# Other places for the filling products, state products and weight conversions at the start of a Mamba-2 and PReLU kernel

## The chip, the cores and the metric

The kernel runs on one core of one Trainium2 chip. The metric is device time in microseconds of one execution, the median of several runs. TensorE (PE) makes matrix products into PSUM banks, VectorE (DVE), ScalarE (ACT) and GpSimd (POOL) do the elementwise work, and SyncE (SP) issues most of the loads. A float32 matrix product is recorded as two passes, so the counts of the profile are twice those of the program.

## The reference

The first part is a Mamba-2 recurrence over 4 batches, 8 heads and 768 positions, with head size 32 and 16 state numbers. The second is a feed-forward layer with a leaky slope per hidden unit (PReLU), on 3072 tokens of 256 numbers with 2048 hidden units.

```python
# per chunk of positions, with cum the running sum of log(clip(a, 1e-6, 1)):
M       = (C @ B.T) * exp(cum_i - cum_j) * causal
y       = M @ x + (C @ state) * exp(cum)
state   = exp(sum(log_a)) * state + B.T @ (x * exp(cum_last - cum))
# then, with x = y laid out as tokens x 256:
h = x @ w_in
g = maximum(h, 0) + alpha * minimum(h, 0)
out = g @ w_out
```

## The kernel before

The kernel takes chunks of 128 positions, two at a time (a "pair", 12 in all). Two pairs make a group of 512 tokens for the feed-forward layer. Only the first group's start concerns us: pairs 0 and 1, then hidden blocks f = 0 to 3 of the first group in halves, and then a loop over f = 4 to 15 that makes `hidden(0, f)`, converts one more piece of the weights, and adds `output(f - 4)`. The three later groups are computed by another, denser scheme that the change does not touch.

The order of instructions on each engine is the order in the program. Tiles in PSUM come from three pools: `ss` (two banks), `hp` (two banks, `spare()` gives one of them) and single banks.

The weights arrive as float64 in 16 pieces of 512 KB (in the order w_in 0, 1, 2, w_out 0, w_in 3, w_out 1, ...) and are converted to float32 by hand. `convert_a` is the first part (ScalarE, then a clamp on GpSimd), `convert_b` the second (VectorE), and `convert` ends with an addition, mostly on GpSimd:

```python
    def convert_a(dst, src, sg):
        ...
        nc.scalar.activation(out=t.bitcast(F32), in_=hi.bitcast(F32), func=ACTF.Abs, scale=0.125)   # L218
        nc.gpsimd.tensor_scalar(out=t..., in0=t..., scalar1=F64_INF, scalar2=F64_ZERO, ...)         # L220
        if sg is None:
            nc.scalar.activation(out=g, in_=half, func=ACTF.Copy, ...)                              # L225
        for i in range(2 if sg is not None else 0):                                                 # w_out
            nc.scalar.activation(out=g[:, i], in_=half[:, i], func=ACTF.Identity, ...)              # L228
    def convert_b(dst, src, sg):
        nc.vector.tensor_single_scalar(out=r, in_=hi, scalar=SIGN, op=ALU.bitwise_and)              # L238
        nc.vector.scalar_tensor_tensor(out=r, in0=t, scalar=3, in1=r, ...)                          # L239
    def convert(dst, src, sg, halves=(nc.gpsimd,)):
        ...
            eng.tensor_tensor(out=d[:, ks], in0=r[:, ks], in1=g.bitcast(U32)[:, ks], op=ALU.add)    # L261

    def convert_next(first=True, **kw):
        i = done[0]
        if i < len(pieces):
            convert(*pieces[i], **kw)
            if first and i and i + 2 < len(pieces):
                convert_a(*pieces[i + 2])
            if loaded[0] == i + 6:
                load_next()
        done[0] += 1
```

`keep_warm` makes products of ones whose results nobody uses; they only keep TensorE occupied:

```python
    def keep_warm(to, n, cols=2 * Q):                       # Q = 128
        for i in range(n):
            nc.tensor.matmul(to[:, :cols], warm[:, :P], warm[:, :cols], start=True, stop=True, ...)  # L270
```

A pair is a generator that is advanced stage by stage with `ssm(gp)`. The parts of it that matter (cut):

```python
        tp = spare() if gp == 1 else ss_tile()
        if gp == 0:
            keep_warm(tp, 1, Q)
        ...                                    # transposes of B and C (L470), bc copied by ScalarE (L473),
                                               # cz = bc masked (L482, L485)
        if gp == 0:
            keep_warm(rows_turn(0, held.pop("pr"))[:, HT:], 5, Q)   # rows_turn: two transposes into one bank,
            yield                                                   # copied by ScalarE (prt, alpha)
        bn = bns.pop(gp) if gp in bns else pair_loads(gp)           # GpSimd, L386
        if gp == 1:
            c_decayed()                                             # GpSimd, L488
            dps = spare()
            ahead[1] = spread(z, 1, lambda w: ss_tile())            # TensorE, L407
        ...
            decays(0)                                               # VectorE scans, L433
            if gp:
                yield
            if gp != 1:
                decays(1)
        def added(dps): ...                                         # state products, TensorE, L532
        def states(dps): ...                                        # VectorE or ScalarE (L541, L544), then sm (L547)
        ...
        if gp == 0:
            gram = products_bc()                                    # CB products, TensorE, L561
            dps = added(spare())
            yield
            c_decayed()
            times(dec[:, :, :2], one_less(gram))                    # one_less: ScalarE, L569; times: GpSimd, L573
        elif gp == 1:
            free = dps[:, HT:]                                      # the upper half of the state products' bank
            dps = added(dps)
            decays(1)
            gram = products_bc()
            keep_warm(free, 2)
            g0 = one_less(gram)
            states(dps)
            times(dec[:, :, :2], g0)
        ...                                                         # VectorE multiplies dec by CB, L600
        y = [...]
        if gp < 2:
            keep_warm(y[0].rearrange("p k t -> p (k t)"), 2)
        ...                                                         # y products (L616, L623), copied to xT (L630)
```

`hidden_two(g, f, t0, hp)` makes two hidden blocks for 256 tokens (products L657, ScalarE L663) and returns a function that does VectorE's part (L669). `hidden` is the same for one block of 512 tokens (L642, L645, L646). `slopes(alpha)` makes the slopes' tables with five small operations on GpSimd (L308 to L317). The order of the start:

```python
    ssm(0)
    convert_a(*pieces[0]); ssm(0); convert_b(*pieces[0]); ssm(0); convert_a(*pieces[1]); ssm(1)
    convert_next(halves=(nc.vector, nc.gpsimd))
    ssm(0)
    ssm(1)
    slopes(alpha)
    prelus = [hidden_two(0, 0, 0, spare())]
    convert_a(*pieces[2])
    convert_next(first=False)
    ssm(1)
    convert_a(*pieces[3])
    prelus.append(hidden_two(0, 2, 0, spare()))
    for rest in prelus:
        rest()
    convert_next()
    ssm(1)
    convert_next(first=False)
    for rest in [hidden_two(0, f, 2 * Q, spare()) for f in range(0, FIRST, 2)]:
        rest()
    identity_bank()                                                 # ScalarE, L333
    convert_a(*pieces[5])
    convert_next()
    for f in range(FIRST, NF):
        ...
```

Of the kernel before, what the change touches and what calls it, by code (L numbers as in the profile page):

```python
# [22 lines left out]
def kernel(  # L23
# [33 lines left out]
    Q = 128  # L57
# [16 lines left out]
    HT = GT // 2  # L74
# [18 lines left out]
    gp = ctx.enter_context(tc.tile_pool(name="gp", bufs=16))  # L93
# [113 lines left out]
    def convert_a(dst, src, sg):  # L207

        if src.dtype == F32:
            return  # L210
        raw = raws.pop(id(dst))
        hi = raw[:, :, :, 1]
        half = raw.rearrange("p k w t -> p k (w t)").bitcast(U16)
        half = half.rearrange("p k (w t) -> p k w t", t=4)[:, :, :, 1]
        t = wtp.tile([P, 2, WQ], U32, name="wt")
        g = wtp.tile([P, 2, WQ], F32, name="wg")

        nc.scalar.activation(out=t.bitcast(F32), in_=hi.bitcast(F32), func=ACTF.Abs, scale=0.125)  # L218

        nc.gpsimd.tensor_scalar(out=t.bitcast(F32), in0=t.bitcast(F32), scalar1=F64_INF,  # L220
                            scalar2=F64_ZERO, op0=ALU.min, op1=ALU.max)


        if sg is None:
            nc.scalar.activation(out=g, in_=half, func=ACTF.Copy, scale=2.0**-11, bias=2.0**25)  # L225
        for i in range(2 if sg is not None else 0):
            f = slice(sg + i, sg + i + 1)
            nc.scalar.activation(out=g[:, i], in_=half[:, i], func=ACTF.Identity,  # L228
                                 scale=g_mul[:, f], bias=g_add[:, f])
        parts[id(dst)] = hi, t, g  # L230
# [36 lines left out]
    def keep_warm(to, n, cols=2 * Q):  # L267

        for i in range(n):
            nc.tensor.matmul(to[:, :cols], warm[:, :P], warm[:, :cols], start=True, stop=True,  # L270
                             skip_group_check=True)
# [27 lines left out]
    alpha = const.tile([P, NF], F32, name="alpha")  # L299
# [6 lines left out]
    def slopes(alp):  # L306
        over = const.tile([P, NF], F32, name="over")
        nc.gpsimd.tensor_scalar(out=over, in0=alp, scalar1=1.0, scalar2=None, op0=ALU.is_gt)  # L308
        nc.gpsimd.tensor_scalar(out=s_mul, in0=over, scalar1=-2.0, scalar2=1.0, op0=ALU.mult,
                                op1=ALU.add)  # L310
        nc.gpsimd.tensor_tensor(out=s_alpha, in0=alp, in1=s_mul, op=ALU.mult)
        if moe_w_out.dtype == F32:
            nc.vector.tensor_single_scalar(out=s_out, in_=s_mul.bitcast(U32), scalar=SIGN,
                                           op=ALU.bitwise_and)
        else:
            for o, by in ((g_mul, 2.0**-11), (g_add, 2.0**25)):
                nc.gpsimd.tensor_scalar(out=o, in0=s_mul, scalar1=by, scalar2=None, op0=ALU.mult)  # L317
# [8 lines left out]
    held = {}  # L326
# [38 lines left out]
    def rows_turn(i, pr):  # L365

        ps = ss_tile()
        nc.tensor.transpose(ps[:, :RW], pr, ident[:RW, :RW])
        if i == 0:
            nc.tensor.transpose(ps[:, RW : RW + NF], al_n, ident[:NF, :NF])  # L370
        t = bat.tile([P, RW], F32, name="prt")
        nc.scalar.copy(out=t, in_=ps[:, :RW])
        if i == 0:
            nc.scalar.copy(out=alpha, in_=ps[:, RW : RW + NF])
        prt[i] = t
        return ps

    def pair_loads(gp):

# [33 lines left out]
    def spare():  # L413

        return ps_h.tile([P, GT], F32, name="hp", tag="hp")

    def pair(gp):
# [7 lines left out]
        def decays(k):  # L425

            if abc:
                for w in range(2):
                    half_decays(k, w)
                return  # L430
            for w, t in enumerate(ahead.pop(k, None) or spread(z, k)):
                ws = slice(512 * w, 512 * w + 512)
                nc.vector.tensor_tensor_scan(out=dv[:, k, ws], data0=t, data1=ident_h[:, ws],  # L433
                                             initial=0.0, op0=ALU.mult, op1=ALU.add)

        def half_decays(k, w):
            for i in range(2):
                hs = slice((2 * w + i) * 2 * Q, (2 * w + i + 1) * 2 * Q)
                nc.vector.tensor_tensor_scan(out=dv[:, k, hs], data0=abc[k][:, hs],  # L439
                                             data1=ident_p[0], initial=0.0, op0=ALU.mult,  # L440
                                             op1=ALU.add)
# [22 lines left out]

        tp = spare() if gp == 1 else ss_tile()
        if gp == 0:
            keep_warm(tp, 1, Q)
        for i in range(2):
            for k in range(2):
                nc.tensor.transpose(tp[:, (2 * i + k) * P : (2 * i + k + 1) * P], nat[:, i, k],  # L470
# [7 lines left out]
        def spread_c():  # L478
            for e in range(2):
                o = cz[:, e].rearrange("p k t -> p (k t)")  # L480
                if gp == 0 and e == 1:
                    nc.gpsimd.tensor_scalar(out=o, in0=ct, scalar1=par[:, e : e + 1],  # L482
                                            scalar2=None, op0=ALU.mult)
                else:
                    nc.scalar.mul(o, ct, par[:, e : e + 1])  # L485

        def c_decayed():
            nc.gpsimd.tensor_tensor(out=cd.rearrange("p k t -> p (k t)"), in0=ct, in1=pf,  # L488
                                    op=ALU.mult)

        fine = gp >= 2 * GC // 2
        if not fine:
            spread_c()
        if gp == 0:
            keep_warm(rows_turn(0, held.pop("pr"))[:, HT:], 5, Q)
            yield
        bn = bns.pop(gp) if gp in bns else pair_loads(gp)
        if gp == 1:
            c_decayed()
            dps = spare()  # L500
            ahead[1] = spread(z, 1, lambda w: ss_tile())
        elif gp:
            yield

        if fine:
            for k in range(2):
                for w in range(2):
                    half_decays(k, w)
                    if k == 1 and w == 1:
                        spread_c()  # L510
                    yield
        else:
            decays(0)
            if gp:
                yield
            if gp != 1:
                decays(1)

# [6 lines left out]
        def added(dps):  # L527
            dps = dps.rearrange("p (k m) -> p k m", m=P)
            for k in range(nk):
                for w in range(KC):  # L530
                    ws = slice(64 * w, 64 * w + 64)
                    nc.tensor.matmul(dps[ws, k], bn[:, k, ws], xt[:, k, w * P : (w + 1) * P],  # L532
                                     start=True, stop=True, tile_position=(0, 64 * w),
                                     skip_group_check=True)
            return dps

        def states(dps):
            for k in range(nk):
# [35 lines left out]

        if gp == 0:
            gram = products_bc()
            dps = added(spare())
            yield
            c_decayed()
            times(dec[:, :, :2], one_less(gram))  # L580
        elif gp == 1:
            free = dps[:, HT:]
            dps = added(dps)
            decays(1)
            gram = products_bc()
            keep_warm(free, 2)
            g0 = one_less(gram)
            states(dps)
            times(dec[:, :, :2], g0)
        else:  # L590
            if not fine:
                yield
            states(added(ss_tile()))
# [3 lines that stand above are left out]
# [10 lines left out]

        y = [ss_tile()[:, : 2 * Q].rearrange("p (k t) -> p k t", k=2) for w in range(KC)]
        if gp < 2:
            keep_warm(y[0].rearrange("p k t -> p (k t)"), 2)  # L610
        begun = False
        for k in range(2):
            if st[k] is not None:
# [284 lines left out]
    def ssm(gp, stages=1):  # L898

        if gp not in pairs:  # L900
            pairs[gp] = pair(gp)
        for i in range(stages):
            next(pairs[gp], None)


    pieces = in_pieces[:2]
# [9 lines left out]
# [11 lines that stand above are left out]
# [13 lines left out]
    FIRST = 4  # L940
# [4 lines left out]
    ssm(0)  # L945
    convert_a(*pieces[1])
    ssm(1)
    convert_next(halves=(nc.vector, nc.gpsimd))
    ssm(0)
    ssm(1)  # L950
    slopes(alpha)
    prelus = [hidden_two(0, 0, 0, spare())]
    convert_a(*pieces[2])
    convert_next(first=False)
    ssm(1)
    convert_a(*pieces[3])
    prelus.append(hidden_two(0, 2, 0, spare()))
    for rest in prelus:
        rest()
    convert_next()  # L960
    ssm(1)
    convert_next(first=False)
    for rest in [hidden_two(0, f, 2 * Q, spare()) for f in range(0, FIRST, 2)]:
        rest()
    identity_bank()
    convert_a(*pieces[5])
    convert_next()
# [108 lines left out]
```

## Time and profile before

| | |
|---|---|
| time, median of 3 runs | 378.24 us (378.05 to 378.95) |
| span of the profiled run | 377.2 us, 6178 instructions |
| TensorE busy | 367.2 us, 97% |
| VectorE, ScalarE, GpSimd busy | 241.5 (64%), 179.5 (48%), 203.2 us (54%) |
| loads and stores | 30.71 MB, mean 81 GB/s |
| mean granted clock of TensorE | 0.994 |

A matrix product's end is modelled, so a busy TensorE isn't TensorE at its peak, and the share of busy time is a mean over stages with different limits. Where a line of the profile ends in square brackets, it gives the idle time of the engine just before that instruction and what ended it. L numbers are lines of the program; a line that stands in a helper covers all uses of that helper. In the chain and in timelines the first two numbers are the start and the duration in us.

### The profile page before, as it was taken

How to read it: one execution, taken by the hardware profiler on the slowest of the kernel's cores; microseconds unless marked ns; L12 is line 12 of the kernel's file. 1: busy time of each engine (PE TensorE's matmuls, PEld its weight loads, DVE VectorE, ACT ScalarE, POOL GpSimd, SP SyncE). 2: the span in 40 equal slices, each digit the busy share in tenths (PEclk: the TensorE clock that was granted, in tenths of full speed). 3: DMA queues.
4: the chain of work that ended last, by engine and by line, in shares of the span. 5: the costliest groups of instructions: out<-in, count | busy, mean ns of one | idle time of the engine just before them, and what ended most of it. 6: DMA issues, size and time to landing. Idle time of an engine off the chain costs nothing.

```text
span 377.2 us, 6178 instructions
## 1 busy us (share of the span) xinstructions
PE 367.2 (97%) x2223; PEld 295.5 (78%) x2223; DVE 241.5 (64%) x461; ACT 179.5 (48%) x384; POOL 203.2 (54%) x212
## 2 busy tenths in 40 slices
PE   7999999999999999999999999999999999999996
PEld 6767566668778788788788788888788788888884
DVE  7777699967636737747737847647856734543364
ACT  1466756525344445545435535525625525543541
POOL 4764476679766846445456345356364355254512
PEclk9899999999999999999999999999999999999999
DMA  7999697921008901001901901901711000001003
GB/s 141 186 225 346 162 272 171 180 70 56 30 0 156 179 2 54 5 0 30 180 3 30 179 2 29 180 2 28 140 44 21 9 0 15 17 0 30 1 0 83
DMA packets 121878, 30.71 MB, mean 81 GB/s; under 512 B 93736, under 2 KB 117752, under 8 KB 121848
## 3 DMA queue, kind: packets, MB, share of 16 engines
q1 hardware_dynamic: 116736, 29.74, 35.4%
q10 hardware_dynamic: 5112, 0.59, 1.1%
q8 instruction: 17, 0.28, 0.3%
q14 instruction: 13, 0.11, 0.1%
HBM read 26.98 MB, written 3.34 MB: 80 GB/s over the span
## 4 chain that ended last, share of the span: by engine, by line
PE 84%; DVE 5%; SPq 4%; DMA 2%; ACT 2%; issue 1%; ACTq 0%; POOLq 0%; DVEq 0%
PE hp L766 33%; PE bank L741 32%; PE bank L680 5%; PE hp L642 3%; PE ss L623 2%; PE ss L561 2%; SPq L165 2%; SPq L163 1%; DMA raw<-in_moe_w_in_dram 1%; PE ss L616 1%; DVE dec L439 1%; PE ss L532 1%; DMA nat<-in_B_dram 1%; PE hp L561 1%; PE hp L657 1%
## 5 line engine op out<-in xcount | busy, mean ns | idle before, releaser
L809 POOL TENSOR_TENSOR gt<-gt 128x512 f32<-128x512 f32 x58 | 73.6, 1270 | 31.8 <-DVE gt L751 24.8
L751 DVE SCALAR_TENSOR_TENSOR gt<-hp,s_mul,gt 128x256 f32<-128x256 f32 x120 | 52.5, 479 | 47.8 <-ACT gt L749 46.8
L741 PE MATMUL bank<-gt,w_out 128*128 128x256 f32 x320 | 82.5, 382 | 0.4 <-ACT o_sb L687 0.4
L749 ACT ACTIVATE gt<-hp,s_alpha 128x256 f32<-128x256 f32 x120 | 50.3, 470 | 47.2 <-PE hp L766 32.9
L741 PEld LDWEIGHTS bank<-gt,w_out 128*128 128x128 f32 x320 | 60.0, 190 | 11.2 <-issue 2.3
L800 POOL TENSOR_TENSOR gt<-gt 128x512 f32<-128x512 f32 x20 | 25.4, 1270 | 78.3 <-DVE gt L751 78.3
L741 PE MATMUL bank<-gt,ws 128*128 128x256 f32 x240 | 58.3, 379 | 0.0
L741 PEld LDWEIGHTS bank<-gt,ws 128*128 128x128 f32 x240 | 45.1, 190 | 5.8
L439 DVE TENSOR_TENSOR_SCAN dec<-abc,bank 128x256 f32<-128x256 f32 x80 | 48.0, 660 | 0.0
L766 PE MATMUL hp<-xs,w_in 128*128 128x256 f32 x160 | 42.9, 390 | 0.0
L766 PE MATMUL hp<-xT,w_in 128*128 128x256 f32 x160 | 41.9, 384 | 0.0
L766 PE MATMUL hp<-xs,ws 128*128 128x256 f32 x160 | 41.1, 379 | 0.0
L785 DVE TENSOR_TENSOR hp<-hp,u 128x512 f32<-128x512 f32 x20 | 14.0, 700 | 39.7 <-ACT u L783 39.7
L774 ACT COPY m<-hp 128x512 f32<-128x512 f32 x20 | 11.7, 586 | 51.5 <-PE hp L766 51.5
L766 PEld LDWEIGHTS hp<-xs,w_in 128*128 128x128 f32 x160 | 28.7, 189 | 7.7 <-issue 3.3
L766 PEld LDWEIGHTS hp<-xs,ws 128*128 128x128 f32 x160 | 30.4, 190 | 4.1
L766 PEld LDWEIGHTS hp<-xT,w_in 128*128 128x128 f32 x160 | 29.7, 190 | 5.0 <-issue 1.4
L680 PEld LDWEIGHTS bank<-w_out,gt 128*128 128x128 f32 x128 | 24.2, 190 | 9.6 <-issue 5.4
L680 PE MATMUL bank<-w_out,gt 128*128 128x256 f32 x128 | 30.6, 381 | 0.6 <-POOL w_out L261 0.6
L789 DVE TENSOR_TENSOR c<-hp,m 128x512 f32<-128x512 f32 x20 | 13.6, 681 | 19.3 <-PE hp L766 19.3
L642 PE MATMUL hp<-xT,w_in 128*128 128x512 f32 x48 | 23.2, 605 | 0.0
L783 ACT COPY u<-hp 128x512 f32<-128x512 f32 x20 | 11.7, 585 | 23.0 <-PE hp L766 23.0
(155 smaller groups left out, 557.1 us busy)
## 6 DMA issues: line engine op xcount, KB each, us to landing
abc<-z SPq DMA_DIRECT2D x20, 512.0 KB, 4.9
raw<-in_moe_w_in_dram SPq DMA_DIRECT2D x8, 512.0 KB, 5.5
raw<-in_moe_w_out_dram SPq DMA_DIRECT2D x8, 512.0 KB, 6.8
xt<-in_x_dram SPq DMA_DIRECT2D x24, 128.0 KB, 3.3
out_dram<-o_sb SPq DMA_DIRECT2D x32, 64.0 KB, 1.9
nat<-in_B_dram SPq DMA_DIRECT2D x22, 64.0 KB, 2.7
nat<-in_C_dram SPq DMA_DIRECT2D x22, 64.0 KB, 3.5
ap<-pf SPq DMA_DIRECT2D x11, 128.0 KB
```

The source lines that it names most:

```text
L439: nc.vector.tensor_tensor_scan(out=dv[:, k, hs], data0=abc[k][:, hs], data1=ident_p[0], initial=0.0, op0=ALU.mult, op1=ALU.add)
L642: nc.tensor.matmul(hp, w_in[:, k, f * P : (f + 1) * P], xts[g][:, k], start=(k == 0), stop=(k == KC - 1))
L680: nc.tensor.matmul(pos[0][t // 2][:, t % 2], gt[:, t * Q : (t + 1) * Q], w_out[:, f], start=(f == 0 and t % 2 == 0), stop=(f == NF - 1), s ...
L741: nc.tensor.matmul(ms[g][i][:, h], w, blocks[g, z][n][:, p], start=(q == 0 and h == 0), stop=(q == NQ - 1), skip_group_check=True)
L749: nc.scalar.mul(o[:, p], h[:, p], s_alpha[:, fs[p]])
L751: nc.vector.scalar_tensor_tensor(out=o[:, p], in0=h[:, p], scalar=s_mul[:, fs[p]], in1=o[:, p], op0=ALU.mult, op1=ALU.max)
L766: nc.tensor.matmul(to[:, p], w(2 * z + p), b, start=start and p == 0, stop=True, skip_group_check=True)
L774: nc.scalar.copy(out=m1, in_=A)
L785: nc.vector.tensor_tensor(out=Y, in0=Y, in1=u2, op=ALU.add)
L789: nc.vector.tensor_tensor(out=c22, in0=A, in1=m5, op=ALU.add)
L800: nc.gpsimd.tensor_tensor(out=tc_, in0=g22, in1=g12, op=ALU.subtract)
L809: eng.tensor_tensor(out=o, in0=x0, in1=x1, op=ALU.subtract)
```

## The change

It moves work at the start of the first group. The products that only fill time get banks of their own, or go: six go to a spare bank right after the two transposes of `rows_turn`, rather than five to the bank of those transposes; three instead of one stand ahead of the first pair's transposes; the two in the upper half of the second pair's state bank go; and one of two ahead of the second pair's y goes. The second pair's state products (`added`) are made earlier, before the first projection. The slopes are made before the end of piece 0. The first parts of pieces 2, 3 and 4 and the second parts of pieces 1 to 3 stand in other places among the second pair's stages and the projections. The aim is that TensorE isn't left idle in the first two pairs, and that VectorE and GpSimd don't stand behind work that waits. No product that is used, and no load, is added or removed.

```diff
@@ pair
-            keep_warm(tp, 1, Q)
+            keep_warm(tp, 3, Q)
@@
         if gp == 0:
-            keep_warm(rows_turn(0, held.pop("pr"))[:, HT:], 5, Q)
+            rows_turn(0, held.pop("pr"))
+            dps = spare()
+            keep_warm(dps, 6, Q)
             yield
@@   (added() and its neighbours are defined before the decays)
             decays(0)
+            if gp == 1:
+                dps = added(dps)
             if gp:
                 yield
@@
         if gp == 0:
             gram = products_bc()
-            dps = added(spare())
+            dps = added(dps)
@@
         elif gp == 1:
-            free = dps[:, HT:]
-            dps = added(dps)
             decays(1)
             gram = products_bc()
-            keep_warm(free, 2)
             g0 = one_less(gram)
@@
         if gp < 2:
-            keep_warm(y[0].rearrange("p k t -> p (k t)"), 2)
+            keep_warm(y[0].rearrange("p k t -> p (k t)"), 2 - gp)
@@ the order of the start
     ssm(1)
+    slopes(alpha)
     convert_next(halves=(nc.vector, nc.gpsimd))
     ssm(0)
     ssm(1)
-    slopes(alpha)
     prelus = [hidden_two(0, 0, 0, spare())]
-    convert_a(*pieces[2])
     convert_next(first=False)
     ssm(1)
+    convert_a(*pieces[2])
+    prelus.append(hidden_two(0, 2, 0, spare()))
+    prelus[0]()
+    convert_next(first=False)
+    prelus[1]()
+    ssm(1)
     convert_a(*pieces[3])
-    prelus.append(hidden_two(0, 2, 0, spare()))
-    for rest in prelus:
-        rest()
-    convert_next()
-    ssm(1)
+    prelus = [hidden_two(0, 0, 2 * Q, spare())]
+    prelus[0]()
+    prelus = [hidden_two(0, 2, 2 * Q, spare())]
+    convert_a(*pieces[4])
     convert_next(first=False)
-    for rest in [hidden_two(0, f, 2 * Q, spare()) for f in range(0, FIRST, 2)]:
-        rest()
+    prelus[0]()
     identity_bank()
     convert_a(*pieces[5])
     convert_next()
```

More of the change, by code (lines that the diff above doesn't have):

```diff
@@ L375, in rows_turn @@
         prt[i] = t
-        return ps
     def pair_loads(gp):
@@ L503, in pair @@
             yield
[L505 to L517, printed above, removed]
         nk = 1 if last else 2
@@ L535, in added @@
             return dps
+        if fine:
+            for k in range(2):
+                for w in range(2):
+                    half_decays(k, w)
+                    if k == 1 and w == 1:
+                        spread_c()
+                    yield
+        else:
+            decays(0)
+            if gp == 1:
+                dps = added(dps)
+            if gp:
+                yield
+            if gp != 1:
+                decays(1)
         def states(dps):
```

## The prediction

> **What bounds the kernel now.** I read the page's chain first, then busy time by stage, then the chain in order of time and each engine's timeline of the first 60 us. On the page, the chain that ended last by engine:
>
> ```profile
> PE 84%; DVE 5%; SPq 4%; DMA 2%; ACT 2%; issue 1%; ACTq 0%; POOLq 0%; DVEq 0%
> ```
>
> TensorE carries 84%. The busy time by stage says where it does not:
>
> ```profile
> 10.00:15.00 5.00, 4.82 (x36) 3.67 (x38) 2.75 (x5) 2.05 (x6) 3.43 (x5) 0.66 0.94 169
> ...
> 34.40:60.00 25.60, 24.10 (x98) 14.89 (x97) 20.75 (x37) 19.05 (x35) 14.23 (x17) 1.00 0.83 246
> 60.00:120.00 60.00, 59.55 (x374) 44.80 (x375) 42.13 (x73) 26.63 (x54) 42.26 (x41) 1.00 0.40 78
> ```
>
> The columns after the stretch and its length are busy us of PE, weight loads, DVE, ACT and POOL, granted clock, DMA share and GB/s. From 60 us on TensorE is 99% busy, and the change touches nothing there. So the change is worth what it takes from the first 60 us, and that is passed on to the end one for one. The chain in order of time in those 60 us:
>
> ```profile
> 23.84 4.92 DMA raw<-in_moe_w_in_dram
> ...
> 28.83 0.69 ACT wt L218
> 29.52 0.60 ACT wg L225
> 30.12 0.28 ACT xT L630
> ...
> 30.44 3.73 PE hp L657 x16
> ...
> 39.49 0.58 ACT gt L645
> ...
> 40.09 0.75 DVE gt L646
> ...
> 60.01 0.34 PE bank L616
> ```
>
> After the second pair's projection (L657) it runs over ScalarE to the first slope of block f=4 (L645, starts 39.40 in the timeline), from 40.09 mostly over VectorE and some ScalarE and TensorE until 59.87, and only then on TensorE for good. So the number to predict is how much earlier L645 and L646 of block 4 come. Before that, three delays. First, the clock, us by us:
>
> ```profile
> 10.00:11.00 1.00, 0.82 (x7) 0.82 (x8) 0.87 (x2) 0.75 (x4) 0.42 (x1) 1.00 0.98 336
> 11.00:12.00 1.00, 1.00 (x10) 0.78 (x12) 0.21 (x1) 0.62 (x2) 0.77 (x2) 0.63 1.37 222
> 12.00:13.00 1.00, 1.00 (x12) 1.00 (x13) 0.49 (x1) 0.00 (x0) 1.00 (x2) 0.50 0.46 51
> ```
>
> It halves at about 11.26 (0.63 in that us) and is back at about 14.68 (0.66 in 14 to 15). The first pair's 8 CB products (L561) take 11.66 to 13.8, 2.2 us; the second pair's take 22.56 to 23.7, 1.14. Second, VectorE:
>
> ```profile
> 21.29 1.20 DVE L433 TENSOR_TENSOR_SCAN dec<-ss,ident_h 128x512 f32<-128x512 f32 x1
> 24.81 0.73 DVE L544 SCALAR_TENSOR_TENSOR state<-state,ap,hp 128x128 f32<-128x128 f32 x2 [2.32 <-PE hp L270]
> ```
>
> It waits 2.32 us not for the state products (L532, 21.98 to 22.6) but for filling products put in the other half of their bank. Third, GpSimd:
>
> ```profile
> 20.71 0.25 POOL L308 TENSOR_SCALAR over<-alpha 128x16 f32<-128x16 f32 x1
> ...
> 23.63 0.61 POOL L220 TENSOR_SCALAR wt<-wt 128x512 f32<-128x512 f32 x1 [1.63 <-ACT wt L218]
> 24.32 1.27 POOL L261 TENSOR_TENSOR w_in<-wr,wg 128x512 uint32<-128x512 uint32 x1
> ```
>
> Piece 1 of w_in is finished only at 25.59, behind the slopes (1.28 us) and piece 2's clamp, which waits for ScalarE; the projection of f=2,3 waits for it until 25.68.
>
> **What the Trainium skill says.** "TensorE: Matmul & The Clock Gate", Part 1, gives half clock after an idle window of about 3.4 us, windows running free. The trace agrees on the length: 11.26 to 14.68 is 3.42 us. It gives no share of activity at which a window counts as idle. In the window ahead (7.84 to 11.26) I count some 2.1 us of products, so a busy share near 60% was not enough. "PSUM — Partial Sum Buffer", the section on bank collisions, says accesses of two engines must be kept apart by bank, not by address: that is the 2.32 us. Its section on engine and sequencer instructions calls ScalarE, VectorE and GpSimd queues strict FIFO; I lean on that below, and the delay of piece 1 behind piece 2's clamp agrees.
>
> **The change, part by part.** Estimates are chained from the durations above.
>
> Start. Six fillings go to a free hp bank straight after the alpha transpose (9.0), instead of five that wait for alpha's copy until 10.18. At 0.107 us a pass, 12 passes end at 10.3; the CB products start when GpSimd's cz is ready (10.42), so 10.5 instead of 11.66, and at full clock end at 11.7 instead of 13.8. The extra two ahead of the transposes lie in a wait for the nat load (0.9). But bn, in GpSimd's FIFO behind a clamp, still ends at 12.98, and VectorE is in piece 0 until 12.48. So the first multiplication by decays starts at 12.5 instead of 13.81, the third ends near 14.95 instead of 16.16, sm near 15.75 instead of 16.40. First y products: 15.9 instead of 16.94, gain 1.0.
>
> Second pair up to its y. The transposes could start at 17.4 instead of 18.37, but the last C load was issued at 13.28, and 4.6 us (median to landing) make 17.9. So spreading k=1 starts at 18.55 instead of 18.96, the scans at 19.75 instead of 20.15. Slopes now stand ahead of piece 0's GpSimd half: 18.5 instead of 17.95; then bn 19.15, cd 20.1, piece 1 at 21.4 instead of 25.59. State products come first at 19.65 to 20.25, projection of f=0,1 until 22.2, CB until 23.35, projection of f=2,3 at once until 25.3 (before: 27.6, after 0.92 of waiting). VectorE: scans to 22.1, states to 22.85 (before 25.54, the 2.32 gone), three multiplications 23.25 to 25.1 (before to 27.33). GpSimd's own ends at 25.0 (before 27.58). With one filling for two, y begins at 25.75 instead of 28.44, and the second half's projection 2.0 later at 27.75 instead of 30.44. Gain here 2.7.
>
> From there to block 4. Part of it is given back. Piece 4's first part stood on ScalarE (28.83 to 30.1) ahead of xT; it now stands behind the last L663. From that L663 to L645 was 39.40 − 34.20 = 5.20 us of ScalarE back to back (0.73 for two L663, 0.30 bank, 0.57+1.04 piece 5, 0.57+0.57 piece 6, 0.60 bc, 0.82 cz); now 0.57+0.57 more, 6.34. L663 starts at 31.5 instead of 34.20, so L645 at 37.85 instead of 39.40: gain 1.5. GpSimd gives the same: its clamp of piece 4 stands ahead of finishing w_out piece 3 and waits for ScalarE (33.0), so w_out is done at 34.9 (before 34.41) and output(0) starts at 34.95 instead of 36.16, gain 1.2. Piece 5 behind block 4 on VectorE gives output(2) at 42.25 instead of 43.79. Sum: 1.5 us, 376.7.
>
> **The rivals.** (a) The half clock moves instead of going. With early CB products TensorE idles from 11.7 to 13.05 for bn, so the window 11.26 to 14.68 holds some 0.4 + 0.6 + 0.9 = 1.9 us, about 55%, no more than the window that halved the clock before. For it: that count. Against: before, 0.6 us of the count were transposes waiting for loads, and what counts as activity isn't visible; and the phase may differ. Fillings (0.86) and y (1.4) of pair 0 would then run at half speed, y of pair 0 ends at 18.75, projection of f=0.. at 28.6, L645 at 38.8: gain 0.6, 377.6. I give it 0.35. (b) Loads take over: the queue issues back to back until 23.84, whatever compute does, piece 4 lands at 28.77 and DMA is about fully busy until 39. For it: this wait is on the chain now. Against: piece 4 is wanted at 32.3 and piece 5 at 33.8 in the new order, piece 6 at 35.4; at 370 GB/s a piece takes 1.4 us, and with the last of them in at 39.0 I estimate piece 6 at 33.5. If it bites, a gain of about 1.0: 377.2. (c) ScalarE's and GpSimd's new order costs more than I count, since piece 3's second part now stands behind the half projection of f=0,1 and piece 4's clamp ahead of it: no gain or 0.3 lost, 378.5. (d) The 2.7 us come through whole, if the chain by VectorE has slack I don't see: 375.5.
>
> **Range and chances.** The sum and the rivals (a), (c) and (d), with (b) falling between: 0.45 × 376.7 + 0.35 × 377.6 + 0.1 × 378.4 + 0.1 × 375.5 = 377.1. The sum itself is the likeliest single value, so I say 376.9, with 375.6 (all of the 2.7) to 378.3 (nothing gained). The three runs before span 0.9. Two per cent is 7.6 us, more than all the delays named; it can't be gained, and nothing costs as much.
>
> **What would show it.** Right: the L544 wait for L270 gone, piece 1 finished by about 21.5, y of pair 1 near 25.8, L645 of block 4 near 37.9, clamp of piece 4 ahead of w_out piece 3 with TensorE waiting near 34, and the same lag at 60 us as at the end. Wrong: clock 0.5 somewhere in 14.7 to 18.1 (rival a); ScalarE's wt waiting for raw loads after 30 us (b); L645 at 39 or later with a full clock (c), or at 37 or earlier (d).

## The result and the profile after

The changed kernel takes 378.25 us (median of 4 runs, 377.88 to 378.76) against 378.44 us for the kernel before, also of 4 runs. The ratio is 0.9995, with a 95% interval of 0.9978 to 1.0013. In a later and larger set (22 runs of it, 376.71 to 379.45) the ratio was 0.9989, interval 0.9974 to 1.0003. So the likeliest gain is about 0.1%, and neither set can tell it from zero. The prediction's sum was a gain of 1.5 us (0.4%), and its stated time 376.9 us.

The profiled run has a span of 376.5 us, against 377.2 before. Of the kernel before, the profiled run was the longest of its set (378.95 us, where the others took 378.05 to 378.65), so differences between the two profiles overstate what the medians gain by about 0.5 us. Busy time by stage of the changed kernel, with the same columns as before (stretch, length, busy us of PE, weight loads, DVE, ACT and POOL, granted clock, DMA share, GB/s):

```profile
10.00:15.00 5.00, 3.39 (x45) 2.56 (x44) 3.95 (x8) 2.98 (x6) 4.01 (x6) 1.00 1.09 186
34.40:60.00 25.60, 23.38 (x104) 14.70 (x108) 19.95 (x35) 16.98 (x30) 14.53 (x17) 1.00 0.87 256
60.00:120.00 60.00, 59.56 (x370) 44.84 (x370) 41.88 (x72) 26.68 (x54) 43.06 (x41) 1.00 0.41 80
```

The clock is full from 10 to 15 us (0.66 before). TensorE is less busy there because its products take less time: the first pair's CB products take 1.14 us (10.28 to 11.42), before 2.2. From 60 us on TensorE is as busy as before (59.56 of 60 us, 59.55 before). Between 34.4 and 60 us all three of TensorE, VectorE and ScalarE have more idle time than before (ScalarE 8.6 us, before 6.6): something keeps them waiting. VectorE's timeline of the changed kernel shows that the wait of 2.32 us for filling products is gone:

```profile
20.78 1.19 DVE L432 TENSOR_TENSOR_SCAN dec<-ss,ident_h 128x512 f32<-128x512 f32 x1
21.90 0.70 DVE L547 SCALAR_TENSOR_TENSOR state<-state,ap,hp 128x128 f32<-128x128 f32 x2
```

The states follow the scans at once, at 21.90 instead of 24.81. The chain in order of time shows where the new wait is:

```profile
26.75 0.38 ACT xT L630
...
27.18 0.18 PE hp L657
27.36 8.67 DMA raw<-in_moe_w_in_dram
...
36.69 0.66 ACT wg L225
...
38.68 0.67 ACT gt L645
39.37 0.75 DVE gt L646
...
59.30 0.34 PE bank L616
```

xT of the second pair comes at 26.75 instead of 30.12, and the projection behind it at 27.18 instead of 30.44: that is 3.3 us gained, more than the 2.7 predicted. Then the chain leaves TensorE for a load: a piece of w_in issued at 27.36, which lands at 36.03. It is piece 6, for f=8 and 9, far ahead of its use on TensorE; but its first part stands in ScalarE's queue ahead of the slopes of block 4. The chain puts a product (L657) ahead of this load, but the load queue's own timeline shows the issue following 0.1 us after that of the third pair's decays (abc):

```profile
25.53 1.72 SPq L136 DMA_DIRECT2D abc<-z  x2
27.36 3.75 SPq L202 DMA_DIRECT2D raw<-in_moe_w_in_dram  x1
```

ScalarE's timeline:

```profile
30.93 0.84 ACT L663 ACTIVATE gt<-hp,s_alpha 128x256 f32<-128x256 f32 x2 [0.89 <-PE hp L657]
...
33.66 1.12 ACT L228 ACTIVATE wg<-raw,g_add,g_mul 128x256 f32<-128x256 uint16 x2
36.11 0.67 ACT L218 ACTIVATE wt<-raw 128x512 f32<-128x512 f32 x1 [1.33 <-DMA raw<-in_moe_w_in_dram]
36.69 0.66 ACT L225 ACTIVATE wg<-raw 128x512 f32<-128x512 uint16 x1
...
38.67 0.67 ACT L645 ACTIVATE gt<-hp,s_alpha 128x512 f32<-128x512 f32 x1
```

It stands still for 1.33 us. L645 of block 4 starts at 38.67 instead of 39.40, and that 0.7 us is what is left of 3.3 at 60 us (59.30 against 60.01) and at the end (376.5 against 377.2).

### The profile page after: what moved, and what is told of

Its sections match the earlier page's. It is cut to its first block, busy times and chain, and to the rows that moved or that the text cites. A ratio compares the mean times of both kernels' runs of the same rounds, so it can differ in the third digit from the quotient of the medians.

```text
span 376.5 us, 6178 instructions
## 1 busy us (share of the span) xinstructions
PE 365.5 (97%) x2223; PEld 294.0 (78%) x2223; DVE 242.2 (64%) x461; ACT 179.8 (48%) x384; POOL 203.7 (54%) x212
## 4 chain that ended last, share of the span: by engine, by line
PE 85%; DVE 5%; DMA 3%; POOL 2%; ACT 2%; issue 1%; ACTq 1%; POOLq 0%; DVEq 0%
PE hp L766 33%; PE bank L741 32%; PE bank L680 5%; PE hp L642 3%; PE ss L623 2%; DMA raw<-in_moe_w_in_dram 2%; PE ss L564 2%; PE ss L616 1%; DVE dec L438 1%; PE ss L519 1%; DMA nat<-in_B_dram 1%; PE hp L657 1%; PE hp L564 1%; PE ss L469 1%; DVE wr L239 1%
## 5 line engine op out<-in xcount | busy, mean ns | idle before, releaser
L809 POOL TENSOR_TENSOR gt<-gt 128x512 f32<-128x512 f32 x58 | 73.7, 1271 | 31.7 <-DVE gt L751 24.8
```

Source lines behind the costliest of these rows:

```text
L809: eng.tensor_tensor(out=o, in0=x0, in1=x1, op=ALU.subtract)
```

## The experiments

**Theory 1:** the first two pairs are faster as predicted, and loads take the gain back, above all piece 6, which the new order wants some 2 us earlier. **Theory 2**, the prediction's rival (c): the new order of ScalarE and GpSimd itself takes it back. Every kernel below computes the full result; times are medians, ratios are to the kernel before in the same set of runs (its medians there lie between 378.41 and 378.87), and L645 is the start of the slopes of block 4 in the profiled run.

| kernel | time, us (runs) | ratio [95% interval] | span, us | L645, us |
|---|---|---|---|---|
| before | 378.24 (3) | | 377.2 | 39.40 |
| changed | 378.25 (4) | 0.9995 [0.9978, 1.0013] | 376.5 | 38.67 |
| e1: decays' loads later | 377.01 (14) | 0.9952 [0.9933, 0.9972] | 375.2 | 37.33 |
| e2: the same in the kernel before | 378.75 (14) | 0.9997 [0.9970, 1.0025] | 377.6 | 39.79 |
| e3: pairs only | 379.69 (20) | 1.0017 [0.9996, 1.0039] | 378.3 | 40.52 |
| e4: order only | 378.98 (12) | 1.0015 [0.9995, 1.0035] | 377.2 | 39.38 |
| e5: e1, first parts earlier | 376.19 (10) | 0.9923 [0.9890, 0.9956] | 374.2 | 36.38 |
| e6: e1 without fillings | 377.25 (18) | 0.9946 [0.9925, 0.9966] | 375.6 | 37.81 |
| e7: before, x loads later | 378.42 (22) | 0.9975 [0.9957, 0.9992] | 376.4 | 38.48 |
| e8: changed, one more load | 379.67 (12) | 1.0008 [0.9982, 1.0034] | 378.2 | 40.32 |
| e9: changed again | 378.37 (22) | 0.9989 [0.9974, 1.0003] | 375.2 | 37.38 |
| e10: before again | 378.85 (1) | | 377.1 | 39.30 |
| e11: e5, x loads later too | 375.59 (6) | 0.9895 [0.9848, 0.9943] | 374.2 | 36.35 |

**e1 and e2: the decays' loads behind pieces 6 and 7.** The third pair's decays come in two loads of 512 KB, used first near 41 us. They stood ahead of piece 6 in the load queue.

```diff
-    load_spread(2, *divmod(4, CPB))      # ahead of piece 6
 ...
     convert_next(first=False)            # frees piece 1, and issues the load of piece 7
+    load_spread(2, *divmod(4, CPB))
```

> The changed kernel, with one thing moved: the two 512 KB loads of the third pair's decays (abc), first used near 41 us, are issued after pieces 6 and 7 of the weights instead of ahead of piece 6. Theory 1 (the gain was given back to loads: ScalarE stood 1.33 us for piece 6, which landed at 36.07): that wait goes, L645 of block 4 starts at 37.4 (36.9 to 37.8) instead of 38.67, the span is 375.2 instead of 376.5, and the time about 0.5% under the kernel before. Theory 2 (ScalarE's and GpSimd's new order costs it, rival c): L645 stays at 38.5 or later, or comes earlier with the span unchanged at 376.3 to 376.7.

> The kernel before, with the same two loads moved behind pieces 6 and 7. Theory 1: nothing in the kernel before waited for piece 6, so L645 of block 4 stays within 0.3 us of 39.40 and the span within 0.4 of 377.2; the time is the same as before within 0.15%. If it is as much faster as the changed kernel with this move, the loads alone are the bound and the change adds nothing to it.

ScalarE's timeline of e1, at the same place:

```profile
33.73 1.12 ACT L228 ACTIVATE wg<-raw,g_add,g_mul 128x256 f32<-128x256 uint16 x2
34.75 0.68 ACT L218 ACTIVATE wt<-raw 128x512 f32<-128x512 f32 x1
35.32 0.69 ACT L225 ACTIVATE wg<-raw 128x512 f32<-128x512 uint16 x1
```

The wait is gone, L645 starts at 37.33, the span is 375.2 and the ratio 0.9952, all as theory 1 had it. Its interval (0.9933 to 0.9972) and that of the 22 runs of the changed kernel (0.9974 to 1.0003) do not touch. In e2 the same move gains nothing: the kernel before came to piece 6 only at 36.84 and didn't wait for it. (L645 is 0.39 us later in e2's profile, a little more than the 0.3 expected.) So the change and this move are worth something only together. e2's profile also shows what held the kernel before:

```profile
29.26 0.67 ACT L218 ACTIVATE wt<-raw 128x512 f32<-128x512 f32 x1 [1.40 <-DMA raw<-in_moe_w_in_dram]
...
30.41 0.34 ACT L630 COPY xT<-bank 128x256 f32<-128x256 f32 x1
```

In this run TensorE kept full clock in the first pair, yet xT came no earlier: it stood behind the first part of piece 4, which had not landed until 29.2, and TensorE waited 1.31 us for xT.

**e3 and e4: each half of the change alone.** e3 takes the pairs of the changed kernel (fillings, state products) with the old order of the start; e4 the other way round.

```diff
 # e3: the body of pair() as changed, the code from FIRST = 4 on as before
 # e4: the body of pair() as before, the code from FIRST = 4 on as changed
```

> Only the half of the change inside a pair (fillings in other banks, fewer of them, state products of pair 1 ahead), with the old order of slopes and conversions. Theory 1: full clock from 11 to 15 us, the 2.3 us wait of the states gone, but the projection of f=2,3 still waits for piece 1 (until about 25.3), and xT behind the first part of piece 4, whose load lands at 28.8: L657 of the second half starts at 30.2 to 30.5 as before, L645 at 39.2 to 39.5, gain in the span under 0.3. Theory 2 (the new order is the loss and the pairs are the gain): L645 at 37.5 to 38.5, span 375.3 to 376.2.

> Only the new order of slopes and conversions, with the pairs as before. Theory 1: half clock near 11.3 to 14.7 and the 2.3 us wait of the states as before (they start at 24.8), y of pair 1 at about 27.4 instead of 28.4, L657 of the second half at about 29.3, L663 at 33.1, and with 6.34 us of ScalarE behind it L645 at 39.4: no gain, span 376.9 to 377.4. Theory 2: L645 at 40 or later, slower by 0.5 us or more.

e4 came as expected at its end (L645 39.38). Its clock stayed full, so the states, still behind fillings (a wait of 1.65 us), start at 23.67 and not at 24.8. e3 came out worse than either theory: L645 at 40.52. Busy time by us in e3:

```profile
24.00:25.00 1.00, 0.00 (x0) 0.00 (x0) 1.00 (x3) 1.00 (x3) 0.92 (x2) 1.00 0.84 119
25.00:26.00 1.00, 0.48 (x1) 0.40 (x2) 0.73 (x2) 1.00 (x3) 1.00 (x2) 0.83 1.04 258
26.00:27.00 1.00, 1.00 (x4) 0.81 (x3) 0.00 (x0) 0.04 (x1) 1.00 (x2) 0.50 0.87 317
```

With faster pairs but piece 1 as late as ever (25.5), TensorE idles 2.52 us, and the clock halves: the projection of f=2,3 takes 3.68 us instead of 1.97. The two fillings that were taken away had stood in that gap; no run has the pairs of e3 with these two put back, so that their absence let the clock halve is not shown by itself. Eleven of e3's 20 runs have a mean clock of 0.995 or less, against five of the 22 of the changed kernel in e9. So neither half gains alone, and in e3 TensorE waits for piece 1.

**e8: a load that nobody reads, ahead of piece 6.**

```diff
     load_spread(2, *divmod(4, CPB))
+    nc.sync.dma_start(out=w_out[:, NF - 4 :]...,          # overwritten later, as before
+                      in_=pieces[8][1].bitcast(U32))      # 512 KB
```

> The changed kernel with one more load of 512 KB, which nobody reads, ahead of piece 6. Theory 1: piece 6 lands 1.4 to 1.6 us later, ScalarE waits about 2.8 instead of 1.33, L645 at 40.1 instead of 38.67, span 377.9, time 0.4% above the changed kernel's, slower than the kernel before by 0.3%. Theory 2 (loads are hidden): no change, span 376.2 to 376.8.

ScalarE in e8:

```profile
37.77 0.67 ACT L218 ACTIVATE wt<-raw 128x512 f32<-128x512 f32 x1 [2.78 <-DMA raw<-in_moe_w_in_dram]
```

The wait grows from 1.33 to 2.78 us, L645 moves to 40.32 and the span to 378.2. In the times the effect is less clear. The median is 1.3 us above the 378.37 of e9, or 1.0 us when each is taken against the kernel before in its own set, and the intervals of the two ratios overlap; nor is e8's ratio clear of 1, so "slower than the kernel before by 0.3%" was not confirmed.

**e9 and e10: both kernels again.**

> The changed kernel once more, with more rounds, for the size of its gain. Theory 1: ScalarE again waits for piece 6 near 35 to 36 us, for 1 to 2 us; L645 of block 4 at 38.2 to 39.2; 0.0 to 0.25% under the kernel before. If the wait was of that one run, L645 at 37.4 and 0.4 to 0.5% under.

> The kernel before once more, for its clock and its wait for piece 4. If the half clock at 11 to 15 us depends on where a window falls, as the two kernels with its pairs that kept full clock suggest, it may be there or not; either way xT and the second half's projection come behind the first part of piece 4, which lands at 28.5 to 29.5, and L645 is at 39.2 to 40.0.

In e9's profiled run ScalarE did not wait for piece 6 at all: L645 at 37.38, span 375.2. That run took 376.95 us, one of the fastest of 22 (376.71 to 379.45; median 378.37). So the wait changes from run to run: the profile has no wait, as the second expectation says, and the median has the small gain of the first. e1's 14 runs lie between 376.66 and 377.52 but for one of 379.01; their fastest is as fast as the changed kernel's fastest. So with the decays out of the way nearly every run is as fast as the changed kernel's runs without the wait. That the other runs of e9 waited for this load I infer from this; they have no profile. A lower clock isn't the reason for most of them: the 17 runs of e9 with a mean clock of 0.998 or more have a median of 378.21, and 13 of e1's 14 have that clock too.

**e7: x of the third pair behind piece 5, in the kernel before.** x is read in runs of 32 numbers, and is first used at 44.80 us here.

```diff
-    load_pair(2, False)                  # B, C, x of pair 2
+    load_pair(2, False, False)           # B and C
     load_next(2)                         # pieces 4 and 5
+    for k in range(2):
+        load_x(loads["p", 2][2], k, 0, slice((4 + k) * Q, (5 + k) * Q))
```

> The kernel before with the two loads of the third pair's x, first used near 45 us, issued after piece 5 instead of ahead of piece 4. If piece 4's landing at 28.8 to 29.3 bounds the kernel before, it lands near 26 and its first part is done before xT: L657 of the second half at 29.8 with full clock (e2 had 30.81) or 30.4 with half clock, L645 at 38.7 or 39.3, the time 0.1 to 0.3% lower. If TensorE and VectorE bound it, nothing changes: within 0.1%.

ScalarE in e7 (line numbers are 4 higher here):

```profile
27.24 0.67 ACT L222 ACTIVATE wt<-raw 128x512 f32<-128x512 f32 x1
27.81 0.69 ACT L229 ACTIVATE wg<-raw 128x512 f32<-128x512 uint16 x1
28.84 0.37 ACT L634 COPY xT<-bank 128x256 f32<-128x256 f32 x1 [0.35 <-PE bank L627]
```

Piece 4 is done before xT and L645 is at 38.48; e2, also at full clock, had 39.79 with piece 4 late. The kernel before gains 0.25% (0.08 to 0.43%) by the order of two loads alone, more than the change is likely to give. In e10, against what was expected, piece 4 was in time (28.32) with half clock, and TensorE came last by 0.35 us. So before, in these profiles, piece 4 and a first pair slowed by half clock stood within about an us of each other, and taking one away left the other.

**e6: what the fillings are worth.** e1 without any filling in the first two pairs.

```diff
-            keep_warm(tp, 3, Q)
-            keep_warm(dps, 6, Q)
-            keep_warm(y[0]..., 2 - gp)
```

> e1 without any filling product in the first two pairs (those at the very start stay). If the fillings are worth their place: half clock for one window or more between 8 and 20 us, y of pair 1 0.7 to 2 us later than e1's 25.25, and with ScalarE behind it L645 later by as much: span 375.9 to 377.2. If they do nothing that matters: the same L645 as e1's 37.33 within 0.3, span 375.0 to 375.5.

```profile
10.00:11.00 1.00, 0.69 (x12) 0.67 (x16) 1.00 (x2) 0.56 (x1) 0.26 (x1) 0.94 1.02 382
11.00:12.00 1.00, 0.91 (x12) 0.18 (x4) 0.52 (x2) 0.78 (x3) 0.80 (x1) 0.50 1.36 219
...
17.00:18.00 1.00, 1.00 (x32) 0.95 (x24) 1.00 (x2) 0.00 (x0) 0.86 (x5) 0.65 1.03 305
```

The clock halves from about 10.9 to 17.7 us (6.8 us; 3.4 in the kernel before). L645 comes 0.5 us later than in e1 and the span is 0.4 us longer: less than expected if they matter, more than if they don't. Most of the half-speed products seem to hide behind other engines: GpSimd works from 11.20 to 19.28 with hardly a gap, in e6 as in the changed kernel.

**e5 and e11: a version that is faster than both.** With the loads out of the way, ScalarE from the last L663 to L645 is the path. e5 moves the first parts of pieces 2, 3 and 4 into ScalarE's idle times and finishes piece 3 earlier; e11 moves the x loads too, behind piece 8.

```diff
+    convert_a(*pieces[2])
     prelus = [hidden_two(0, 0, 0, spare())]
     convert_next(first=False)
     load_spread(2, *divmod(4, CPB))
     ssm(1)
-    convert_a(*pieces[2])
+    convert_a(*pieces[3])
     prelus.append(hidden_two(0, 2, 0, spare()))
     ...
     ssm(1)
-    convert_a(*pieces[3])
+    convert_a(*pieces[4])
     prelus = [hidden_two(0, 0, 2 * Q, spare())]
+    convert_next(first=False)
     prelus[0]()
     prelus = [hidden_two(0, 2, 2 * Q, spare())]
-    convert_a(*pieces[4])
-    convert_next(first=False)
     prelus[0]()
```

> The changed kernel with the decays' loads behind piece 7 as in e1, and the first parts of pieces 2, 3 and 4 on ScalarE each one stage earlier, in its idle times (19.5 to 21.9, 23.5 to 24.9, 27.4 to 29.3), and piece 3 finished ahead of the second half's slopes. Theory 1 (with the loads out of the way, ScalarE from the last L663 to L645 is the path, 6.34 us of it, of which 1.14 are piece 4): L645 of block 4 at 36.2 (35.9 to 36.8), output(0) without its wait of 1.44 us, span 374.1 (373.8 to 374.8), time 0.7 to 0.8% under the kernel before. If piece 4 lands after 30 or piece 6 after 34.5, loads bound it again: L645 at 36.8 to 37.3, span 374.6 to 375.2.

> e5 with the third pair's two x loads (first used near 43 us) issued after piece 8 instead of ahead of piece 4. If what is left of the scatter of e5's times (375.34 to 378.86) is again pieces that land late, it narrows and the median falls to 375.5 to 375.9, 0.75 to 0.9% under the kernel before; L645 of block 4 at 36.0 to 36.4 and no wait for a load on ScalarE after 20 us. If the scatter has another cause, the range stays over 2 us and the median at 376.0 to 376.4.

ScalarE in e5, last L663 to L645:

```profile
31.16 0.84 ACT L663 ACTIVATE gt<-hp,s_alpha 128x256 f32<-128x256 f32 x2 [0.89 <-PE hp L657]
31.89 0.39 ACT L333 COPY bank<-ident_h 128x256 f32<-128x256 f32 x1
...
36.38 0.67 ACT L645 ACTIVATE gt<-hp,s_alpha 128x512 f32<-128x512 f32 x1
```

5.22 us, as in the kernel before (5.20); with piece 4 in it, it is 6.33 in e1 (31.00 to 37.33). e5 is 0.77% faster than the kernel before. Its runs spread from 375.34 to 378.86; with x out of the way as well (e11), six runs lie between 375.10 and 375.96, median 375.59, 1.05% faster (0.57 to 1.52%; 0.75 to 0.9 was expected). The intervals of e1, e5 and e11 overlap: that e5 and e11 are ahead of e1 is shown by their profiles (L645 earlier by 0.95 and 0.98 us, the span by 1.0), not by the times. One expectation failed: in e11's profile ScalarE waits 1.00 us for piece 2 at 20.28 and 0.20 for piece 4. Both lie in its idle time, and L645 stays at 36.35.

## Why the prediction was wrong

**What bounds the kernel** was read half right. The number to predict was indeed L645 of block 4: 0.73 us earlier there, 0.71 at 60 us, 0.7 at the end. But the line of 4.92 us of DMA at 23.84, which the prediction quoted from the chain, says that piece 4's load comes ahead of xT, and the prediction then named three delays, none of them a load; it came back to this wait only in rival (b). e2 and e7 show that it was a fourth.

**Start:** right. CB products from 10.28 (predicted 10.5) at full clock, y of pair 0 at 15.77 (15.9).

**Second pair:** right in every step, and a little small. The transposes came at 17.21, not at 17.9: I took a C load issued at 13.28 and a median of 4.6 us to landing, and this run issued it at 12.46. y at 25.18 (25.75), projection at 27.18 (27.75), gain 3.3 instead of 2.7. Part of this is gain over a run before that had half clock; e2 and e4 have the old pairs at full clock, and their y of pair 1 starts 0.7 and 1.1 us before the 28.44 of the kernel before (27.78 and 27.31).

**To block 4:** this is the step that failed. "L663 starts at 31.5 instead of 34.20, so L645 at 37.85": L663 started at 30.93, and 6.34 us later would be 37.27, but L645 came at 38.67, 7.74 us later. e1 and e9, with no wait for piece 6, have 37.33 and 37.38. So ScalarE's sum of work was right, and without the wait the gain of the profiled run would have been 2.0 us. What the step had wrong is that ScalarE works there without waiting: the sum had no term for the load of piece 6, which cost 1.33 us in the profiled run, nothing in e9's, and 2.78 with one more load ahead of it (e8). GpSimd's side was right: the clamp of piece 4 ahead of w_out, and TensorE waiting for it 1.45 us until 34.50 (predicted 34.95). It did not set the end: e1 keeps that wait (1.44 us) and gains all the same.

**The rivals.** (a) did not come: TensorE idles from 11.4 to 13.0 and the clock stays full. In the six other profiles with the new pairs and all their fillings it is full until 19 us as well, while it halves near 11 us in two of five profiles with the old ones. Some unprofiled runs of the changed kernel have a mean clock of 0.994, the same as the two with the half clock, so it seems not to be gone for good, though where they lost it isn't recorded. The prediction's inference that "a busy share near 60% was not enough" for full clock is no rule: the same products with nearly the same gaps kept full clock in e2, e4 and e7. (b) is what happened, and the weighing of it was wrong: "at 370 GB/s ... I estimate piece 6 at 33.5" takes pieces to land one after another at a steady 370 GB/s. The queue issued piece 6 only at 27.36, after 1 MB of decays that nobody needed before 41 us, and DMA moved 254 GB/s from 27 to 30 us. Its cost of "a gain of about 1.0" was near the 0.7 of the profiled run. (c) did not come: e1 keeps that order and loses nothing by it. (d) did not come either: even e1, without the wait, has L645 at 37.33 and 377.01 us, where (d) has 37 or earlier and 375.5.

**Range and chances.** 378.25 lies at the edge of the range, 375.6 to 378.3, and that 2% was out of reach held. The chances of the sum, (a), (c) and (d) add up to 1, so (b) had none of its own, in a stretch where the profile shows DMA about fully busy until 39 us. The stated 376.9 is neither the sum (376.7) nor the weighted mean (377.1), and the mean takes 378.4 for (c) where its text has 378.5. And the delays were read from a profile whose run took 378.95 us but were taken off the median, 378.24: from 378.95, the sum of 1.5 gives 377.45, and the profiled run of the changed kernel took 378.28. So some 0.7 of the 1.6 us between that run and the sum's 376.7 is this difference, and the rest is close to how late L645 came (38.67, predicted 37.85).

## What to carry to other kernels

When a change makes a stage want its operands earlier, go through the load queue for that stage in order, and give every load the time when it is first used; a load that isn't needed yet and stands ahead of one that is takes the gain. Here the queue did not follow the compute: in the eleven profiles with the same loads ahead of it, piece 4 was issued between 22.99 and 24.07 us, so a stage that gets faster only comes to wait for its load. And the first engine to wait may be one that converts data for much later, if its queue also holds work that is due now.

## What the runs showed that I had not expected

The same load of the same kernel landed at least 1.2 us apart in two runs, more than the change gains: piece 6 landed at 36.03 in one and was there by 34.80 in the other (e9). It was already 1.4 us apart at its issue (27.36 and 25.94): the queue had spent 3.57 us issuing one load of x and 1.17 on a piece of w_out in the first run, 2.62 and 0.47 in the second. The order of e5 with x out of the way narrowed the spread of times from 3.5 us (ten runs of e5) to 0.9 us (six of e11). And the half clock in the first pair comes and goes: with the same fillings and nearly the same gaps TensorE was halved at 11 us in two runs (before, e10) and not in three (e2, e4, e7). Where it halves in these profiles it stays so for about 3.4 us (before, e10, e3) or about twice that (e6, 6.8 us).
